# Block transposes of q and k in a fused retention and gated-MLP kernel: TensorE or the DMA queue

## The chip, the cores and the metric

One core of a Trainium2 chip runs the kernel. The metric is device time in microseconds (us) for one execution, the median of the runs; lower is better. The engines are named as in the profile: PE (TensorE), PEld (its weight loads), DVE (VectorE), ACT (ScalarE), POOL (GpSimd) and SP (SyncE, which here only issues DMAs; SPq is its queue).

## The reference

```python
# q, k, v: [8, 8, 576, 64] f32 (batch, heads, positions, head_dim)
scores = q @ k.T / sqrt(64)                       # per batch and head
gamma = 1 - 2 ** (-5 - arange(8))                 # per head
ret = scores * where(i >= j, gamma ** (i - j), 0)
x = (ret @ v) with the heads put side by side     # [8, 576, 512]
h = gelu_tanh(x @ w_in)                           # w_in [512, 1024]
u, v = h[..., :512], h[..., 512:]
v_n = (v - mean) / sqrt(var + 1e-6) * g_ln        # over the 512 columns
v_s = w_sg @ v_n + b_sg                           # over positions, w_sg [576, 576]
out = x + (u * v_s) @ w_out                       # f32
```

## The kernel before, in words

**Blocks.** The sequence work is cut into 18 blocks (`NB`). A block is 256 positions by 8 heads: block 0 of each group of nine takes the first 64 positions of four batches, and the other eight take the two halves of the remaining 512 positions of those four batches. The decay is factored into tables `gq` and `gk`, so that the causal retention becomes a product of scaled q and k, a mask, and a running state.

**Steps of a block j.** `load` brings q, k, v in f32 from HBM, issued on SyncE (L87 and L91; 512 KB each). `cast` scales and converts them to bf16 tiles `qb`, `kb`, `vb`, in the loop on POOL (L245, L263). `T(j, part)` turns a block's q or k: eight TensorE transposes (L272) into one PSUM tile `tp`, and one copy to SBUF, on DVE for `qT` and on ACT for `kT` (both by the helper at L245). `Sc` makes the scores from `kT` and `qT` (L296) and masks them on DVE (L300); it is called in two halves, g = 0 and 1. `Z` updates the state (L321), `inter` applies the earlier state to `qT` (L337), `intra` applies the masked scores to v (L348) and copies the result to `xT` on ACT. `V` and `U` are the two halves of the first MLP matmul with gelu (L365, L414); `V` puts the normalisation off by `later(2, stats)` and `later(4, norm)`. `W` mixes over positions (L434, L436), `O` is the last matmul with the residual (L443, L446), the copy to `ob` on ACT (L449) and the store issued on SyncE (L452, L455).

**Order.** The order is written out by hand, engine queue by engine queue, and nothing reorders it. Blocks 0 to 2 are in a straight prologue, which also transposes blocks 3 and 4. The main loop (L603) runs j from 3 to 17; iteration j works on block j, makes the scores of block j + 1, casts block j + 3, loads block j + 4 and transposes block j + 2: q after the first slot of queued work, k near the end. `W` and `O` steps wait in a list and are put in by `run(slots[i])`, one to two at a time. `tick()` is called at the end of `T`, `V`, `U`, `W` and `O`; every deferred step counts these calls and is put into the queues when its count is out.

**Buffers.** `ld` has three buffers for loads, `w2` two for `qb`, `qT` and `kT`, `w3` three for `kb`, `vb` and `ob`. The PSUM pool `psS` has two tiles of the tag `att`, shared by `tp` and by the scores `sc`.

Of the kernel before, what the change touches and what calls it, by code (L numbers as in the profile page):

```python
# [12 lines left out]
BF = mybir.dt.bfloat16  # L13
# [6 lines left out]
def kernel(  # L20
# [12 lines left out]
    nc = tc.nc  # L33
# [3 lines left out]
    KK = H // 2  # L37
# [4 lines left out]
    NB = B // GB * NPG  # L42
# [7 lines left out]
    w2 = ctx.enter_context(tc.tile_pool(name="w2", bufs=2))  # L50
# [11 lines left out]
    def place(j):  # L62

        gr, w = divmod(j, NPG)
        return (gr, None, 0) if w == 0 else (gr, GB * gr + (w - 1) // 2, (w - 1) % 2)

    def chunk(j, c):

        gr, b, half = place(j)
        if b is None:  # L70
            return 2 * gr + c, MID
        return b // 2, (MID + 1) * (b % 2) + 2 * half + c
# [3 lines left out]
    def load(j, parts=(k, q, v)):  # L76
        if j not in loaded:
            loaded[j] = ld.tile([128, 2, H, 2, D], F32, name="qk"), ld.tile([128, H, 2, D], F32, name="vf")
        qk, vf = loaded[j]
        gr, b, half = place(j)  # L80
        for dst, src in ((qk[:, 1], k), (qk[:, 0], q), (vf, v)):
            if src not in parts:
                continue
            if b is None:
                for x in range(GB):
                    eng = nc.scalar if j == 0 and x >= 2 and src is not v else nc.sync
                    eng.dma_start(dst[32 * x:32 * x + 32], src[GB * gr + x, :, :LEAD, :].rearrange(  # L87
                        "h (p a) d -> p h (a d)", a=2))
            else:
                s0 = LEAD + 256 * half  # L90
                nc.sync.dma_start(dst[:], src[b, :, s0:s0 + 256, :].rearrange("h (p a) d -> p h (a d)", a=2))  # L91
# [143 lines left out]
    def tick():  # L235
        for e in pend:
            e[0] -= 1
        while pend and pend[0][0] <= 0:
            pend.pop(0)[1]()

    blk = {}
    xTs, uTs, gTs, vns, zbs = {}, {}, {}, {}, {}

    def copy(eng, o, i):
        (eng.copy if eng is nc.scalar else eng.tensor_copy)(o, i)  # L245

    def cast(j, part, eng):
        s = blk.setdefault(j, {})
        qk, vf = loaded[j]
        b, half = place(j)[1:]  # L250
        kind = 0 if b is None else 1 + half
        if part == "q":
            dst, src, tab = w2.tile([128, 2, H, D], BF, name="qb"), qk[:, 0], gq
        else:
            pool = consts if b is None else w3
            dst = pool.tile([128, 2, H, D], BF, name=part + ("lead" if b is None else "b"))
            src, tab = (qk[:, 1], gk) if part == "k" else (vf[:], None)
        s[part + "b"] = dst
        o = dst[:].rearrange("p a h d -> p h a d")
        if tab is None:  # L260
            copy(eng, o, src)
        else:
            eng.tensor_tensor(o, src, tab[:, kind].rearrange("p a h -> p h a").unsqueeze(3).to_broadcast(  # L263
                [128, H, 2, D]), op=Alu.mult)

    def T(j, part):
        s = blk[j]
        src = s[part + "b"]
        tp = psS.tile([128, 2, KK, 128], BF, name="tp", tag="att")
        for a in range(2):  # L270
            for kk in range(KK):
                nc.tensor.transpose(tp[:, a, kk, :], src[:, a, 2 * kk:2 * kk + 2, :].rearrange("p h d -> p (h d)"),  # L272
                                    ident[:])
        dst = w2.tile([128, 2, KK, 128], BF, name=part + "T")
        s[part + "T"] = dst
        if j == 0 and part == "q":
            nc.vector.tensor_copy(dst[:, :, :2], tp[:, :, :2])
            nc.scalar.copy(dst[:, :, 2:], tp[:, :, 2:])
        else:
            copy(nc.vector if part == "q" else nc.scalar, dst[:], tp[:])  # L280
        tick()

    def Sc(j, g):
        s = blk[j]
        qT, kT = s["qT"], s["kT"]
        if g == 0:
            s["ret"] = w2.tile([128, 2, KK, 2, 128], BF, name="ret")
        sc = [(psD if (j, g) == (0, 1) else psS).tile([128, 2, 2, 128], F32, name="sc",
                                                      tag="d" if (j, g) == (0, 1) else "att") for _ in range(2)]
        for x in range(2):  # L290
            kk = 2 * g + x
            for a in range(2):
                for r in range(2):
                    for c in range(2):
                        rr, cc = slice(64 * r, 64 * r + 64), slice(64 * c, 64 * c + 64)
                        nc.tensor.matmul(sc[r][cc, x, a, :], kT[rr, a, kk, cc], qT[rr, :, kk, cc],  # L296
                                         start=True, stop=True, skip_group_check=True)
        msk = mask[1 if place(j)[1] is None else 0]
        for r in range(2):
            nc.vector.tensor_tensor(s["ret"][:, r, 2 * g:2 * g + 2], sc[r][:],  # L300
                                    msk[:].unsqueeze(1).to_broadcast([128, 2, 2, 128]), op=Alu.mult)
# [3 lines left out]
    def Z(j, c):  # L305

        gr, b, half = place(j)
        if b is None or (half, c) == (1, 1):
            nb = GB * gr if b is None else b + 1
            if c == 0 or nb == GB * (gr + 1):  # L310
                return
            src, lo, n, first = blk[NPG * gr], 32 * (nb % GB), 32, True
            zcur[0] = psZ.tile([128, KK, D], F32, name="zp")
        else:
            src, lo, n, first = blk[j], 64 * c, 64, False
        z, rows = zcur[0], slice(lo, lo + n)
        for a in range(2):
            for kk in range(KK):
                for r in range(2):
                    h = 2 * kk + r  # L320
                    nc.tensor.matmul(z[64 * r:64 * r + 64, kk, :], src["kb"][rows, a, h, :], src["vb"][rows, a, h, :],  # L321
                                     start=(first and a == 0 and kk == 0), stop=True, skip_group_check=True)
        zb = w3.tile([128, KK, D], BF, name="zb")
        copy(nc.scalar if j < 3 else nc.vector, zb[:], z[:])
        zbs[(j, 1) if c == 0 else (j + 1, 0)] = zb
# [14 lines left out]
    def intra(j):  # L340
        s = blk[j]
        ret, vb, ot = s["ret"], s["vb"], s["ot"]
        ks = [(kk, a) for kk in (2, 3, 0, 1) for a in range(2)]
        for kk, a in ks:
            for c in range(2):
                for r in range(2):
                    cc = slice(64 * c, 64 * c + 64)
                    nc.tensor.matmul(ot[c][64 * r:64 * r + 64, kk], vb[cc, a, 2 * kk + r, :],  # L348
                                     ret[cc, r, kk, a, :],
                                     start=(place(j)[1] is None and (kk, a) == ks[0]),  # L350
                                     stop=True, skip_group_check=True)
        for c in range(2):
            p, m = chunk(j, c)
            if p not in xTs:
                xTs[p] = pairp.tile([128, KK, NT * 128], BF, name="xT")
            x = xTs[p][:, :, 128 * m:128 * m + 128].rearrange("p k (t a) -> p k a t", a=2)
            copy(nc.vector if j < 3 and c == 1 else nc.scalar, x, ot[c][:])
# [102 lines left out]
    def run(n):  # L460
        for _ in range(n):
            if wo:
                wo.pop(0)()
# [139 lines left out]
    for j in range(HEAD, NB):  # L603
        nx = j + 1 < NB
        slots = where[share.get(j, 6)]
        more = (lambda *p: load(j + 4, p)) if j + 4 < NB else (lambda *p: None)
        more(q)
        intra(j)
        if nx:
            Sc(j + 1, 0)  # L610
            Z(j + 1, 0)
        if j + 3 < NB:
            cast(j + 3, "q", nc.gpsimd)
        run(slots[0])
        more(k)
        if j + 2 < NB:
            T(j + 2, "q")
        V(j, 0)
        if not nx:
            V(j, 1)  # L620
        run(slots[1])
        U(j, 0)
        more(v)
        if nx:
            inter(j + 1)
            Sc(j + 1, 1)
            Z(j + 1, 1)
            run(slots[2])
            V(j, 1)
        if j + 3 < NB:  # L630
            cast(j + 3, "k", nc.gpsimd)
            cast(j + 3, "v", nc.gpsimd)
        if j + 2 < NB:
            T(j + 2, "k")
        U(j, 1)
        run(slots[3])
        release(j)
# [36 lines left out]
```

## Time and profile before

| what | value |
|---|---|
| median of 3 runs | 234.67 us (234.17 to 237.1) |
| the profiled execution | 234.34 us, of which 232.6 us span |
| TensorE clock granted | 0.995 of full speed |
| busy share PE, PEld, DVE, ACT, POOL | 92%, 67%, 71%, 58%, 56% |
| PE transposes (L272) | 288, of which 144 of q and 144 of k |
| copies of `kT` (ACT) and `qT` (DVE, L245) | 18 at 1008 ns, 17 at 688 ns |
| DMA | 41.59 MB in 64261 packets, mean 179 GB/s |

The span runs from the first to the last instruction of the profiled execution; a little time lies around it. Busy time of PE overlaps between neighbouring groups, so the place that a group takes in the queue is read from the starts of the groups. A row of the timeline gives start, length, engine, source line, operation, what it writes and reads, and how many instructions were merged. A window row gives the window, its length, and the busy time of PE, PEld, DVE, ACT and POOL with the count of instructions, then the clock, the DMA engines' mean busy share and GB/s. A DMA row gives the size and the median time from issue to landing.

### The profile page before, as it was taken

The page shows a single profiled execution, that of the slowest core. Times are in us where ns is not written, and L with a number is a line of the kernel's source. Part 1 is how long each engine was busy: PE and PEld are TensorE (multiplying, and loading weights), DVE is VectorE, ACT ScalarE, POOL GpSimd, SP SyncE. Part 2 cuts the span into 40 slices and gives each one's busy share as a digit, 9 for nine tenths or more (in the row PEclk, how much of TensorE's full clock was granted, in tenths as well). Part 3 has the DMA queues.
Part 4 walks back from the last instruction along what each step waited for, and adds up shares of the span by engine and source line. Part 5 has one row for each costly group of instructions (what it writes and reads, how often), then busy time and mean ns, then how long its engine had stood idle before and what let it go on. Part 6 is the DMA issues. An engine that isn't in the chain of part 4 may idle for free.

```text
span 232.6 us, 8357 instructions
## 1 busy us (share of the span) xinstructions
PE 215.0 (92%) x3603; PEld 154.8 (67%) x3603; DVE 165.8 (71%) x357; ACT 134.7 (58%) x217; POOL 129.4 (56%) x130
## 2 busy tenths in 40 slices
PE   7796879789997999999999899999999999999991
PEld 3344476577776786777768677777777777667760
DVE  5476788688979896579767886779857985566320
ACT  5353568614669464946575757657394739466332
POOL 5298869799958485538555674939381611113000
PEclk9999999999999999999999999999999999999997
DMA  6999999999396993699249922869522003300344
GB/s 167 286 301 297 302 258 275 238 282 268 94 261 204 201 230 65 207 278 291 79 126 299 276 74 66 251 213 287 146 90 93 4 3 111 118 3 0 136 116 159
DMA packets 64261, 41.59 MB, mean 179 GB/s; under 512 B 2208, under 2 KB 58592, under 8 KB 64224
## 3 DMA queue, kind: packets, MB, share of 16 engines
q1 hardware_dynamic: 61664, 39.33, 62.6%
q0 software_dynamic: 1472, 1.20, 3.1%
q10 hardware_dynamic: 1088, 0.52, 1.0%
q8 instruction: 28, 0.46, 0.9%
q14 instruction: 9, 0.07, 0.1%
HBM read 32.79 MB, written 9.44 MB: 182 GB/s over the span
## 4 chain that ended last, share of the span: by engine, by line
PE 67%; ACT 7%; DVE 6%; DMA 6%; POOL 5%; SPq 5%; issue 1%; ACTq 1%; DVEq 0%; POOLq 0%
PE wp L434 15%; PE op L443 13%; PE hv L365 10%; PE hu L414 10%; PE tp L272 5%; SPq L91 5%; DMA wst<-in_moe_w_in_dram 4%; PE op L446 3%; POOL rs L372 3%; PE zp L321 3%; PE sc L296 3%; PE ot L348 3%; PE ot L337 3%; DMA qk<-in_q_dram 2%; DVE bst L376 2%; ACT vnm L393 2%
## 5 line engine op out<-in xcount | busy, mean ns | idle before, releaser
L372 POOL TENSOR_TENSOR rs<-rs,mhalf 128x1 f32<-128x1 f32 x36 | 33.0, 916 | 73.0 <-DVE rs L380 67.9
L300 DVE TENSOR_TENSOR ret<-sc,mask 128x512 bf16<-128x512 f32 x72 | 46.2, 684 | 12.9 <-PE sc L296 12.8
L434 PE MATMUL wp<-wT,vn 128*128 128x288 bf16 x256 | 41.7, 287 | 2.9 <-ACT vn L397 2.8
L436 DVE TENSOR_TENSOR gT<-wp,uT 128x288 bf16<-128x288 f32 x64 | 28.1, 453 | 16.8 <-PE wp L434 14.0
L365 PE MATMUL hv<-w_in,xT 128*128 128x512 bf16 x144 | 36.5, 379 | 2.4 <-ACT xT L245 2.4
L414 PE MATMUL hu<-xT,w_in 128*128 128x128 bf16 x576 | 37.8, 219 | 0.0
L443 PE MATMUL op<-w_out,gT 128*128 128x512 bf16 x144 | 37.1, 380 | 0.0
L414 PEld LDWEIGHTS <-w_in 128*128 128x128 bf16 x576 | 34.0, 98 | 1.9
L368 ACT ACTIVATE vg<-hv 128x512 f32<-128x512 f32 x36 | 21.4, 596 | 22.5 <-PE hv L365 22.3
L376 DVE BATCH_NORM_STATS2 bst<-vg 128x6 f32<-128x512 f32 x36 | 24.8, 689 | 12.1 <-ACT vg L368 11.9
L449 ACT COPY ob<-op 128x512 f32<-128x512 f32 x36 | 20.9, 586 | 20.5 <-PE op L446 18.0
L263 POOL TENSOR_TENSOR kb<-qk,gk 128x1024 bf16<-128x1024 f32 x16 | 31.1, 1941 | 2.8 <-DMA qk<-in_k_dram 2.8
L397 ACT ACTIVATE vn<-vc,rs 128x512 bf16<-128x512 f32 x32 | 23.1, 722 | 14.4 <-POOL rs L372 12.4
L434 PEld LDWEIGHTS <-vn 128*128 128x128 bf16 x256 | 23.8, 98 | 10.7 <-ACT vn L397 3.7
L385 DVE SCALAR_TENSOR_TENSOR vc<-vg,mv,g_bc 128x512 f32<-128x512 f32 x36 | 29.9, 830 | 0.2 <-issue 0.2
L263 POOL TENSOR_TENSOR qb<-qk,gq 128x1024 bf16<-128x1024 f32 x15 | 28.9, 1929 | 0.0
L417 ACT ACTIVATE uT<-hu 128x512 bf16<-128x512 f32 x36 | 21.7, 602 | 11.5 <-PE hu L414 11.5
L245 ACT CAST xT<-ot 128x512 bf16<-128x512 f32 x33 | 22.0, 733 | 1.8 <-PE ot L348 1.6
L245 ACT COPY kT<-tp 128x1024 bf16<-128x1024 bf16 x18 | 18.1, 1008 | 8.3 <-PE tp L272 8.3
L365 PEld LDWEIGHTS <-xT 128*128 128x128 bf16 x144 | 12.8, 98 | 13.7 <-ACT xT L245 4.0
L443 PEld LDWEIGHTS <-gT 128*128 128x128 bf16 x144 | 12.3, 98 | 9.5
L434 PE MATMUL wp<-wL,vnm 128*128 128x288 bf16 x64 | 18.4, 287 | 0.0
(95 smaller groups left out, 290.0 us busy)
## 6 DMA issues: line engine op xcount, KB each, us to landing
qk<-in_k_dram SPq DMA_DIRECT2D x16, 512.0 KB, 8.2
qk<-in_q_dram SPq DMA_DIRECT2D x16, 512.0 KB, 7.5
vf<-in_v_dram SPq DMA_DIRECT2D x16, 512.0 KB, 7.6
out_dram<-ob SPq DMA_DIRECT2D x32, 256.0 KB, 2.5
wst<-in_moe_w_in_dram SPq DMA_DIRECT2D x2, 1024.0 KB, 7.3
vf<-in_v_dram SPq DMA_DIRECT2D x8, 128.0 KB, 4.3
out_dram<-ob SPq DMA_DIRECT2D x8, 128.0 KB, 2.4
qk<-in_k_dram SPq DMA_DIRECT2D x6, 128.0 KB, 3.4
```

Source lines behind the costliest of these rows:

```text
L245: (eng.copy if eng is nc.scalar else eng.tensor_copy)(o, i)
L263: eng.tensor_tensor(o, src, tab[:, kind].rearrange("p a h -> p h a").unsqueeze(3).to_broadcast([128, H, 2, D]), op=Alu.mult)
L300: nc.vector.tensor_tensor(s["ret"][:, r, 2 * g:2 * g + 2], sc[r][:], msk[:].unsqueeze(1).to_broadcast([128, 2, 2, 128]), op=Alu.mult)
L365: nc.tensor.matmul(hv[:], xTs[p][:, kk, 128 * m:128 * m + 128], w_in[:, kk, F2:], start=(kk == 0), stop=(kk == KK - 1))
L372: nc.gpsimd.tensor_tensor(st["rs"][:], st["rs"][:], mhalf[:], op=Alu.pow)
L376: nc.vector.bn_stats(bst[:], vg[:])
L385: nc.vector.scalar_tensor_tensor(vc[:], vg[:], mv[:, 0:1], g_bc[:], op0=Alu.subtract, op1=Alu.mult)
L397: nc.scalar.mul(vn[:], vc[:], rs[:])
L414: nc.tensor.matmul(hu[:, c, :], w_in[:, kk, 128 * c:128 * c + 128], xTs[p][:, kk, 128 * m:128 * m + 128], start=(kk == 0), stop=(kk == KK ...
L434: nc.tensor.matmul(ps[:], vns[p, m][e][:, 128 * c:128 * c + 128], w, start=(x == 0), stop=(x == SB - 1))
L436: nc.vector.tensor_tensor(gTs[p][:, c, col:col + HS], ps[:], uTs[p][:, c, col:col + HS], op=Alu.mult)
L443: nc.tensor.matmul(op[:], gTs[p][:, c, r], w_out[:, c, :], start=(c == 0), stop=False, skip_group_check=True)
```

## The change

In the main loop both calls of `T` are replaced by a new function `turn`, which issues one DMA on SyncE: a transposing DMA that reads the block's bf16 tile in SBUF and writes `qT` or `kT` in SBUF in the same layout as before. No PSUM tile and no copy is used. For q it stands at the start of iteration j, behind the q load of block j + 4 and ahead of `intra(j)`; for k behind the k load of block j + 4, ahead of `V(j, 0)`. `turn` does not call `tick()`. Iterations 3 to 15 have it, so blocks 5 to 17; the prologue's calls of `T` for blocks 0 to 4 stay.

```diff
+    def turn(j, part):
+
+        s = blk[j]
+        s[part + "T"] = dst = w2.tile([128, 2, KK, 128], BF, name=part + "T")
+        nc.sync.dma_start_transpose(dst[:].rearrange("p a k t -> p (a k) t"),
+                                    s[part + "b"][:].rearrange("p a h d -> p (a h d)"))
...
         more(q)
+        if j + 2 < NB:
+            turn(j + 2, "q")
         intra(j)
...
         run(slots[0])
         more(k)
         if j + 2 < NB:
-            T(j + 2, "q")
+            turn(j + 2, "k")
         V(j, 0)
...
             cast(j + 3, "k", nc.gpsimd)
             cast(j + 3, "v", nc.gpsimd)
-        if j + 2 < NB:
-            T(j + 2, "k")
         U(j, 1)
```

The function T stays as it is for blocks 0 to 4:

```python
    def T(j, part):
        ...
        for a in range(2):
            for kk in range(KK):
                nc.tensor.transpose(tp[:, a, kk, :], src[:, a, 2 * kk:2 * kk + 2, :].rearrange("p h d -> p (h d)"),
                                    ident[:])
        dst = w2.tile([128, 2, KK, 128], BF, name=part + "T")
        ...
            copy(nc.vector if part == "q" else nc.scalar, dst[:], tp[:])
        tick()
```

## The prediction

> **What bounds the kernel now.** I read the busy shares first, then the chain that ended last, then windows of the stage that the edit touches, then the DMA view. The page's busy line, its DMA lines and its chain:
>
> ```profile
> PE 215.0 (92%) x3603; PEld 154.8 (67%) x3603; DVE 165.8 (71%) x357; ACT 134.7 (58%) x217; POOL 129.4 (56%) x130
> ...
> DMA  6999999999396993699249922869522003300344
> GB/s 167 286 301 297 302 258 275 238 282 268 94 261 204 201 230 65 207 278 291 79 126 299 276 74 66 251 213 287 146 90 93 4 3 111 118 3 0 136 116 159
> ...
> PE 67%; ACT 7%; DVE 6%; DMA 6%; POOL 5%; SPq 5%; issue 1%; ACTq 1%; DVEq 0%; POOLq 0%
> ```
>
> TensorE is busy for 92% and carries 67% of the chain; no other engine is near it. The DMA engines are the second full resource: near nine tenths up to about 50 us, then in bursts, at most 302 GB/s, and nearly idle after 170 us. The stage of the edit, in windows (columns: window and length, PE, PEld, DVE, ACT, POOL busy, then clock, DMA share, GB/s):
>
> ```profile
> 62.00:84.00 22.00, 20.75 (x395) 15.61 (x391) 18.81 (x39) 15.30 (x25) 14.95 (x13) 1.00 0.83 205
> 118.30:139.00 20.70, 19.67 (x389) 15.31 (x392) 16.25 (x37) 13.14 (x21) 11.79 (x9) 1.00 0.81 218
> 62.20:172.90 110.70, 108.41 (x1961) 81.20 (x1964) 85.95 (x185) 71.68 (x116) 68.47 (x54) 1.00 0.72 190
> ```
>
> From 62.2 to 172.9 us PE is busy 108.41 of 110.7 us at a clock of 1.00, and what is missing lies in the two shorter windows. So here time is what PE's queue costs, and DMA stands at 0.72. The main loop's length comes from the first and the last of its intra groups in that window:
>
> ```profile
> 62.16 0.64 PE L348 MATMUL ot<-ret,vb 64*64 64x128 bf16 x32
> ...
> 172.80 0.64 PE L348 MATMUL ot<-ret,vb 64*64 64x128 bf16 x32
> ```
>
> Ten iterations lie between these starts: (172.80 - 62.16)/10 = 11.06 us each.
>
> **What is removed.** The loop makes blocks 5 to 17 by `turn`: 13 blocks, q and k, so 26 calls of T go, with 208 PE transposes, 13 DVE copies and 13 ACT copies. What one T holds of PE's queue is the distance from its start to the start of what follows:
>
> ```profile
> 109.04 0.61 PE L272 MATMUL tp<-ident,qb 128*128 128x128 bf16 x8
> 109.49 0.81 PE L365 MATMUL hv<-w_in,xT 128*128 128x512 bf16 x3
> ```
>
> That is 0.45 us for eight transposes (the 0.61 us is busy time that overlaps the next group). 26 x 0.45 = 11.7 us. Not all of it is on the path: in two stretches the chain runs through ACT, DVE and POOL while PE has spare time:
>
> ```profile
> 65.81 0.61 ACT vg L368
> ...
> 75.07 0.91 PE wp L434 x6
> ...
> 123.57 0.61 DVE bst L376
> ...
> 132.39 1.04 PE hv L365 x4
> ```
>
> The windows of the transposes alone (PE, DVE, ACT busy) show how many T lie in these:
>
> ```profile
> 65.80:75.10 9.30, 0.61 (x8) 0.00 (x0) 1.00 (x1) 1.00 0.82 241
> 123.60:132.40 8.80, 1.22 (x16) 0.18 (x1) 1.01 (x1) 1.00 1.12 287
> ```
>
> 8 + 16 transposes, three T, so 3 x 0.45 = 1.35 us gain nothing. The first term is -(11.7 - 1.35) = -10.35 us, bounds -10.35 and -11.7. The 26 copies lie on engines at 71% and 58%; I count no gain for them.
>
> **The lost ticks.** T also called tick(), `turn` does not, so the deferred norm steps come up to two calls later: some `bst` groups stand behind one more `gT` on DVE, and some `vn` behind `xT` or `ob` on ACT. Who waits is the matmul group that reads `vn`:
>
> ```profile
> PE wp L434 <- ACT vn L397: 2.8, 2, 1.5
> ```
>
> These two waits total 2.8 us. I take 0, since DVE and ACT also lose their copies; the bounds are -2.8 (waits gone) and +2.8 (doubled).
>
> **What is added: the transfers.** 26 DMA transposes of 128x1024 bf16, 262,144 bytes each, in SyncE's queue between the loads. The built instruction cuts one into 64 tiles of 16 rows by 128 columns: 1,024 source rows of 256 bytes, and in the destination 8,192 pieces of 32 bytes. No row of this trace is a transpose, so I bound it by other transfers:
>
> ```profile
> q1 hardware_dynamic: 61664, 39.33, 62.6%
> ...
> qk<-in_k_dram SPq DMA_DIRECT2D x16, 512.0 KB, 8.2
> ```
>
> By bytes at the best slice, 262,144 / 302 GB/s = 0.87 us. By pieces: a block's load is 1,024 rows of 512 bytes, 524,288 / 302 GB/s = 1.74 us, or 27 ns a row on each of 16 engines. By the mean packet, 0.626 x 16 x 232.6 us / 61,664 = 37.8 ns, and 64 rows on each engine make 2.42 us. If each 32-byte piece cost 27 ns, 512 per engine make 13.9 us. Ends: 0.87 and 13.9 us. The nearest row is the block's load, with as many pieces and twice the bytes, so I take the middle of 0.87 and 1.74: 1.3 us.
>
> The room: an iteration moves 190 GB/s x 11.06 us = 2.10 MB and uses 0.72 x 11.06 = 7.96 us of the DMA engines by their share, 6.96 us at 302 GB/s. After the edit it would last 11.06 - 0.90 = 10.16 us. That leaves 2.2 to 3.2 us, middle 2.7, for two transposes of 1.3 us, 2.6 us. They just fit, so this term is 0. It eats the whole gain once 11 iterations that still load lose 10.35 us, 0.94 each: at (2.2 + 0.94)/2 = 1.6 to (3.2 + 0.94)/2 = 2.1 us a transpose.
>
> **What is added: a wait.** `turn` stands on SyncE behind the load of the same name and, in some iterations, behind an out store that waits for ACT's `ob`. Queued behind it are the v load, the later stores and the next loads; those have a block and more before POOL wants them. For its own operands it waits on POOL's casts, a block ahead, and on PE's reads of the old buffer. What can be late is kT, which PE wants in `Sc(j+2, 0)` one iteration on. Two iterations in which a store holds the k load back, SyncE's rows, then PE's scores:
>
> ```profile
> 144.41 0.43 SPq L91 DMA_DIRECT2D qk<-in_k_dram  x1
> ...
> 153.57 0.43 SPq L91 DMA_DIRECT2D qk<-in_k_dram  x1
> ```
>
> ```profile
> 150.52 0.39 PE L296 MATMUL sc<-qT,kT 64*64 64x128 bf16 x16
> ...
> 161.48 0.39 PE L296 MATMUL sc<-qT,kT 64*64 64x128 bf16 x16
> ```
>
> Their landing, from the DMA view of each issue:
>
> ```profile
> qk<-in_k_dram SPq DMA_DIRECT2D x1, 512.0 KB, 5.3
> ...
> qk<-in_k_dram SPq DMA_DIRECT2D x1, 512.0 KB, 7.0
> ```
>
> From issue to need there are 6.1 and 7.9 us, less 0.45 us for the T that goes in between: 5.7 and 7.5. If the transpose lands 1.3 us after the load ahead of it, that is 6.6 and 8.3: late by 0.9 and 0.8 us. I take four such iterations at 0.85: +3.4 us; the ends are 0 and 11 x 0.85 = 9.4 us. Elsewhere SyncE runs ahead and the block of lead covers it.
>
> **The sum** is made against the profiled execution: 232.6 us of span, 234.34 us in all, 0.33 below the median of 234.67. 234.34 - 10.35 + 0 + 0 + 3.4 = **227.4 us**. Its own range is 222 to 232.
>
> **The rivals.**
>
> *All is hidden.* kT lands in time everywhere and PE's whole 11.7 us go: 234.34 - 11.7 = 222.6 us. For it speak the median load's 8.2 us, which is queueing with its neighbours rather than work; against it the two rows above.
>
> *The DMA engines become the bound.* At 2.42 us a transpose, two take 4.84 us against 2.2 us of room: 2.6 us over in each of 11 loading iterations, 29 us. 234.34 - 10.35 + 29 = 253 us, slower. It decides from 1.6 to 2.1 us a transpose on; stores and loads then land ever later, and PE waits at the scores and POOL at its casts. For it: the share of 1.12 at 287 GB/s in one window, and the first 50 us. Against it: half the bytes per row, and idle engines after 170 us.
>
> *Transposes cost by small pieces.* At 13.9 us each, two take 27.8 us against 2.7: 25.1 x 11 = 276 us, about 500 us in all. Every smaller per-piece cost above the 2.42 us lies between this and 253. Nothing in the trace excludes it, since no transfer here writes 32-byte runs. A rule of the Trainium skill points this way: VectorE: DVE Perf Modes, section "The three transpose paths", has 1309 ns for a 128x128 DMA transpose against 390 ns on TensorE. Eight of them one after another would be an estimated 10.5 us and the kernel about 425 us; no run here shows whether a part of that is a fixed cost paid once.
>
> *The change doesn't do what it says:* the built program has the 26 transposes on SyncE and 208 fewer on PE, so I give this no chance.
>
> **How the numbers follow.** The forecast has 0.45, all hidden 0.13, the DMA bound 0.28, small pieces 0.14. A kernel change here can be told from none at about 2%, 4.7 us. Faster by that is below 230.0: 0.33 of the forecast's 0.45 and all of the first rival, 0.46. Within 2%: the forecast's slow end, 0.12, and the DMA bound's fast end, 0.05, together 0.17. Slower: 0.23 and 0.14, 0.37. Both signs hold much, so the range is wide: 220 us, a little under all hidden, to 275 us, which leaves out the small pieces and little else. The likeliest case's own is 222 to 232.
>
> **What would show it.** Right: the transposes of `tp` end at block 4 (80 PE transposes left), PE's iteration near 10.2 us, landings of `qT` and `kT` of 2 to 8 us, PE waits on `kT` of 0.5 to 1.5 us in about four iterations, a DMA share near 0.9 from 62 to 160 us. Wrong: landings of 10 us and more, long issues on SyncE, PE waiting at L303 in every iteration, or POOL waiting on loads; then the term at fault is the 1.3 us. If PE's iteration stays near 11 us with no such waits, the 0.45 us was not on the path.

## The result, and the profile after

| kernel | median | ratio to before, 95% interval |
|---|---|---|
| before | 234.9 us (20 runs) | |
| the change | 234.41 us (20 runs) | 0.9945 [0.9918, 0.9971] |

The change gains 0.55%, 1.3 us: by the 2% of this measurement, no difference. The ratio, here and below, leaves out the runs that are over 1.5% above the fastest of the same kernel, so it is not the quotient of the medians, here 0.998; gains in us are the ratio's distance from 1 times 234.9. The forecast was 227.4 us. The profile shows that the work did leave PE and that the time came back as waits. The profiled execution of the change took 239.14 us, the longest of its 20, so its waits are at the upper end; the run with a fourth `ob` buffer below has 9.4 us of the same waits in an execution of 233.0 us of span.

The page's busy line, clock line and chain of the change:

```profile
PE 211.0 (89%) x3395; PEld 146.1 (62%) x3395; DVE 159.3 (67%) x344; ACT 123.4 (52%) x204; POOL 129.4 (55%) x130
...
PEclk9999799999999999998899989997999999999999
...
PE 53%; DMA 21%; DVE 8%; POOL 6%; ACT 3%; issue 3%; SPq 3%; ACTq 1%; POOLq 0%; DVEq 0%
```

PE has 208 matmuls fewer (3395 for 3603) but a larger share of idle time, the DMA share of the chain went from 6% to 21%, and the clock, flat before, has dips. Where PE waits now, from the view of waits (engine and line, what ended the wait, us in total, times, longest):

```profile
PE sc L303 <- DMA kT<-kb: 8.7, 5, 2.4
PE sc L303 <- DMA kT<-klead: 2.6, 1, 2.6
PE wp L441 <- ACT vn L404: 2.0, 2, 1.4
```

Six times the scores wait for kT, 11.3 us in all. The kernel before has no such row. What the transfers cost, from the DMA view of the change:

```profile
q1 hardware_dynamic: 89120, 46.15, 87.5%
...
qT<-qb SPq DMA_TRANSPOSE x13, 6.7
kT<-kb SPq DMA_TRANSPOSE x12, 6.1
```

27,456 packets more than before, 1,056 a transpose, and (0.875 x 237.4 - 0.626 x 232.6)/26 = 2.39 us of all 16 engines for one, against 1.3 us in the forecast. This is the sum of the packets' times, and packets overlap: the same share is above 1 in the windows below. So 2.39 us is not the time by which a transpose makes the queue longer. A transpose lands 6.1 to 6.7 us after its issue in the median. One of the waits in order of time, SyncE first and then PE:

```profile
124.34 3.32 SPq L287 DMA_TRANSPOSE qT<-qb  x1
127.75 0.53 SPq L462 DMA_DIRECT2D out_dram<-ob  x1
128.33 0.43 SPq L91 DMA_DIRECT2D qk<-in_k_dram  x1
128.85 3.41 SPq L287 DMA_TRANSPOSE kT<-kb  x1
```

```profile
131.42 0.65 PE L441 MATMUL wp<-wT,vn 128*128 128x288 bf16 x4
132.00 0.64 PE L355 MATMUL ot<-ret,vb 64*64 64x128 bf16 x32
135.00 0.42 PE L303 MATMUL sc<-qT,kT 64*64 64x128 bf16 x16 [2.35 <-DMA kT<-kb]
135.24 0.54 PE L328 MATMUL zp<-vb,kb 64*64 64x64 bf16 x16
135.71 0.42 PE L441 MATMUL wp<-wL,vnm 128*128 128x288 bf16 x1
135.93 1.17 PE L441 MATMUL wp<-wT,vn 128*128 128x288 bf16 x4
```

The issue of the q transpose holds SyncE for 3.32 us, then come a store and the k load, and the k transpose is issued only 3.8 us before PE has nothing left to do (132.64). It lands 6.1 us after its issue, 2.35 us late. After the wait four `wp` matmuls take 1.17 us, where as many took 0.65 us ahead of it: the clock is down for some microseconds. Windows of the change (columns as before; the last three are clock, DMA share and GB/s):

```profile
62.00:84.00 22.00, 18.48 (x351) 13.16 (x350) 16.89 (x36) 12.42 (x21) 13.88 (x12) 1.00 1.20 250
107.00:118.00 11.00, 8.42 (x126) 5.49 (x125) 6.27 (x15) 3.50 (x6) 4.24 (x5) 0.84 1.37 209
...
135.40:140.00 4.60, 4.60 (x47) 2.94 (x38) 2.54 (x5) 0.66 (x2) 0.57 (x1) 0.63 1.17 284
140.00:145.00 5.00, 5.00 (x113) 3.81 (x114) 4.59 (x12) 2.48 (x5) 3.56 (x3) 1.00 1.28 197
```

The three longest waits, 2.58, 2.35 and 2.28 us, are each followed by such a stretch; those of 1.55 and 1.62 us, both in the first row, are not. Between 107 and 173 us four windows have a lower clock: 0.84 in 11 us, 0.92 in 21, 0.92 in 11 and 0.93 in 12. Each length times what its clock lacks to 1 gives 5.2 us in all, an estimate of what the clock cost in this execution if PE was the limit in all of them.

### The profile page after: what moved, and what is told of

Read it like the earlier page. It is cut to its first block, busy times and chain, and to the rows that moved or that the text cites. A ratio compares the mean times of both kernels' runs of the same rounds, so it can differ in the third digit from the quotient of the medians.

```text
span 237.4 us, 7964 instructions
## 1 busy us (share of the span) xinstructions
PE 211.0 (89%) x3395; PEld 146.1 (62%) x3395; DVE 159.3 (67%) x344; ACT 123.4 (52%) x204; POOL 129.4 (55%) x130
## 4 chain that ended last, share of the span: by engine, by line
PE 53%; DMA 21%; DVE 8%; POOL 6%; ACT 3%; issue 3%; SPq 3%; ACTq 1%; POOLq 0%; DVEq 0%
PE wp L441 13%; PE op L450 12%; DMA kT<-kb 10%; PE hv L372 9%; PE hu L421 7%; DMA qk<-in_q_dram 4%; DMA qk<-in_k_dram 4%; DMA kT<-klead 3%; PE op L453 3%; DVE bst L383 3%; PE sc L303 3%; PE zp L328 2%; PE ot L355 2%; DVE vc L392 2%; SPq L91 2%
## 5 line engine op out<-in xcount | busy, mean ns | idle before, releaser
L441 PE MATMUL wp<-wT,vn 128*128 128x288 bf16 x256 | 44.3, 299 | 2.3 <-ACT vn L404 2.0
L372 PE MATMUL hv<-w_in,xT 128*128 128x512 bf16 x144 | 38.0, 391 | 1.4 <-ACT xT L245 1.4
L421 PEld LDWEIGHTS <-w_in 128*128 128x128 bf16 x576 | 34.6, 98 | 5.0
L441 PEld LDWEIGHTS <-vn 128*128 128x128 bf16 x256 | 24.7, 101 | 12.2 <-ACT vn L404 3.2
L392 DVE SCALAR_TENSOR_TENSOR vc<-vg,mv,g_bc 128x512 f32<-128x512 f32 x36 | 31.7, 880 | 0.2 <-issue 0.2
L303 PE MATMUL sc<-qT,kT 64*64 64x128 bf16 x576 | 17.0, 219 | 12.1 <-DMA kT<-kb 8.7
L424 ACT ACTIVATE uT<-hu 128x512 bf16<-128x512 f32 x36 | 21.4, 596 | 11.6 <-PE hu L421 11.3
L372 PEld LDWEIGHTS <-xT 128*128 128x128 bf16 x144 | 13.8, 102 | 14.4 <-ACT xT L245 2.9
L303 PEld LDWEIGHTS <-kT 64*64 64x64 bf16 x576 | 11.8, 106 | 14.9 <-DMA kT<-kb 9.5
L441 PE MATMUL wp<-wL,vnm 128*128 128x288 bf16 x64 | 19.1, 299 | 0.4 <-DVE gT L443 0.4
```

The costliest lines, as they stand in the source:

```text
L372: nc.tensor.matmul(hv[:], xTs[p][:, kk, 128 * m:128 * m + 128], w_in[:, kk, F2:], start=(kk == 0), stop=(kk == KK - 1))
L392: nc.vector.scalar_tensor_tensor(vc[:], vg[:], mv[:, 0:1], g_bc[:], op0=Alu.subtract, op1=Alu.mult)
L421: nc.tensor.matmul(hu[:, c, :], w_in[:, kk, 128 * c:128 * c + 128], xTs[p][:, kk, 128 * m:128 * m + 128], start=(kk == 0), stop=(kk == KK ...
L441: nc.tensor.matmul(ps[:], vns[p, m][e][:, 128 * c:128 * c + 128], w, start=(x == 0), stop=(x == SB - 1))
```

## The experiments

Three theories went in. A: the gain on PE is real and is given back by a late kT. B: the DMA engines are full, so the transfers slow everything, wherever they are issued. C: the transposes were not on the path.

**No transfer.** What the PE work alone is worth.

```diff
...
-        s[part + "T"] = dst = w2.tile([128, 2, KK, 128], BF, name=part + "T")
-        nc.sync.dma_start_transpose(dst[:]..., s[part + "b"][:]...)
+        blk[j][part + "T"] = blk[j - 2][part + "T"]
```

> The changed kernel without its 26 DMA transposes: from block 5 on the scores read the qT and kT tiles of blocks 3 and 4 again, so the output leaves the blocks' own transposed q and k out. It shows what the removed TensorE work is worth when nothing is late. Theory A (the gain is real and is given back in PE's waits for kT and in the lower clock after them): 222.6 to 225 us, 10 to 12 below before, clock 0.99, no wait of PE at the scores. Theory B (the extra transfers fill the DMA engines): the same 222.6 to 225. Theory C (the PE transposes were not on the path, DVE and POOL set the pace): 231 to 235 us.

Measured: 224.94 us, 0.9576 [0.952, 0.9632], clock 1.00, no wait of PE for kT. That is 4.2%, 10.0 us of 234.9, with the 26 copies and the ticks gone as well; theory C falls.

**Transfers that nobody waits for.** T stays everywhere; the transposes run beside it into dead halves of the load buffers.

```diff
+        old = loaded[j][0][:, 0 if part == "q" else 1].rearrange("p h a d -> p (h a d)").bitcast(BF)
+        nc.sync.dma_start_transpose(old[:, :1024]..., blk[j][part + "b"][:]...)
```

> All PE transposes and copies of the kernel before, and beside them the 26 DMA transposes at the places of the change, written into load buffers that are already used up, so that nobody computes with them. (The load that fills that buffer next waits for them.) Theory A: the transfers alone cost little, 234 to 237 us. Theory B: loads and stores are pushed back and the kernel slows by 5 to 12 us, 240 to 247 us, with POOL waiting for loads or ACT for stores. Theory C says nothing of it: 234 to 236 us.

Measured: 238.18 us, 1.010 [1.0024, 1.0176]: 1.0%, some 2.4 us, between A and B and far from B's 5 to 12. The DMA queue is as full as with the change, and the loss shows at the stores (lines of the DMA view and of the waits of this run):

```profile
q1 hardware_dynamic: 89120, 46.15, 90.1%
```

```profile
ACT ob L455 <- DMA out_dram<-ob: 5.0, 4, 1.8
```

ACT waited 0.9 us for stores in the kernel before and 5.0 us here. There are three `ob` buffers, and a store that lands later holds ACT.

**q alone, k alone.** Half of the change each; the other half stays on PE.

```diff
 # q alone
-            turn(j + 2, "k")
...
+            T(j + 2, "k")
 # k alone
-            turn(j + 2, "q")
...
             turn(j + 2, "k")
+            T(j + 2, "q")
```

> Only q goes by DMA, at the place of the change; k stays on PE and ACT as before. 13 transposes of 0.45 us leave PE. Theory A: q stands early in its iteration and lands in time, so half of the gain stays, 5 us: 228 to 231 us, clock 0.99, PE's waits for qT under 2 us in all. Theory B: half of the transfers, half of the loss: 232 to 234 us. Theory C: 232 to 235 us.

> The mirror of q alone: only k goes by DMA, at the place of the change; q stays on PE and DVE. The same 13 transfers and the same 13 x 0.45 us of PE work less as in the run with q alone, which gained 2.5 per cent. Theory A (k's place makes it late): PE waits for kT again, 4 to 11 us, and the kernel takes 231 to 235 us. Theory B (only the count of transfers matters): the same as with q alone, 228 to 230.5 us.

Measured: q alone 229.19 us, 0.9747 [0.9698, 0.9796], with no wait of PE for qT. k alone 231.47 us, 0.9839 [0.98, 0.9877]; the waits for kT in this run:

```profile
PE sc L303 <- DMA kT<-kb: 2.6, 3, 0.9
```

The same 13 transfers and the same PE work gain 2.5% at q's place and 1.6% at k's, and only k's has a wait, so place counts, as A says. (The halves also take their copies off different engines, 13 off DVE for q and 13 off ACT for k; that was not separated.) But the halves together would give 4.1%, and both at once give 0.55%. Without the q transpose ahead of it kT is late by 2.6 us in all, with it by 11.3: what each transpose gains is paid back by what the two together make late.

**Both early.** Same transfers, both ahead of the loads and of the stores of the iteration's slots.

```diff
-        more(q)
         if j + 2 < NB:
             turn(j + 2, "q")
+            turn(j + 2, "k")
+        more(q)
         intra(j)
...
-            turn(j + 2, "k")
```

> Both DMA transposes stand at the start of the iteration, q first, ahead of all three loads of block j + 4 and of the out stores of its slots. The transfers are the same. Theory A: kT is issued some 3 to 6 us earlier and lands before the scores; PE's waits for it go from 11.3 us to under 3, clock 0.99, and the kernel takes 224 to 228 us. Theory B: the DMA engines are as full as before, 232 to 235 us, with the wait moved to the loads. Theory C: 232 to 235 us with no waits at the scores.

Measured: 233.53 us, 0.9824 [0.9754, 0.9893]. The wait for kT is nearly gone, as A had it. The time is unclear: the four runs reach from 230.3 to 236.35 us, between A's band and B's. The waits of the profiled one, 235.45 us, and then ACT and PE about the longest of them:

```profile
PE wp L441 <- ACT vn L404: 6.1, 3, 4.2
...
ACT ob L456 <- DMA out_dram<-ob: 6.0, 3, 4.0
...
PE sc L303 <- DMA kT<-kb: 0.5, 1, 0.5
```

```profile
152.39 0.59 ACT L456 COPY ob<-op 128x512 f32<-128x512 f32 x1 [4.04 <-DMA out_dram<-ob]
152.87 1.32 ACT L245 CAST xT<-ot 128x512 bf16<-128x512 f32 x2
154.03 0.62 ACT L456 COPY ob<-op 128x512 f32<-128x512 f32 x1
154.50 0.76 ACT L404 ACTIVATE vn<-vc,rs 128x512 bf16<-128x512 f32 x1
```

```profile
155.31 0.42 PE L441 MATMUL wp<-wT,vn 128*128 128x288 bf16 x1 [4.17 <-ACT vn L404]
155.52 0.45 PE L441 MATMUL wp<-wL,vnm 128*128 128x288 bf16 x1
155.76 1.91 PE L372 MATMUL hv<-w_in,xT 128*128 128x512 bf16 x4
```

A store lands late, ACT cannot write `ob`, `vn` stands behind it on ACT, and PE waits 4.17 us for `vn`. So in this run the wait moved. Whether the two runs near 231 us have it too is not shown.

**Both early and a fourth `ob` buffer,** with its two controls.

```diff
+    obp = ctx.enter_context(tc.tile_pool(name="obp", bufs=4))
...
-        ob = w3.tile([128, DM], F32, name="ob")
+        ob = obp.tile([128, DM], F32, name="ob")
```

> Both transposes early as in the run before, and four buffers for ob in place of three. With both early PE's wait for kT was gone, and in its place ACT waited 4.0 us once for a store to land before it could write ob, with vn and PE's matmuls behind it. Theory A: this wait was the last large one; it goes, clock 0.99, 226 to 229 us. Theory B (the DMA engines are simply full): the wait shows again elsewhere, at POOL's casts or PE's scores, 231 to 235 us.

> The kernel before with four buffers for ob in place of three, nothing else: the control for the run with both transposes early and four buffers. ACT waited 0.9 us in all for stores in the kernel before, so all theories expect 233 to 236 us, a ratio of 0.995 to 1.002.

> The change in its own places, with four buffers for ob. If the place of kT is the cause and the fourth buffer only removes the wait that follows when kT is early: PE's waits for kT stay near 11 us and the time is that of the change, 233 to 236 us. If the fourth buffer alone brought the gain of the run with both: 228 to 231 us.

| kernel | three `ob` | four `ob` |
|---|---|---|
| before | 1 | 0.9982 [0.994, 1.0023] |
| the change | 0.9945 [0.9918, 0.9971] | 0.9981 [0.9935, 1.0027] |
| both early | 0.9824 [0.9754, 0.9893] | 0.9724 [0.9668, 0.9779] |

The buffer alone does nothing that can be told from noise, before or with the change; the place alone brings 1.8%, unclear against the 2%; both bring 2.8%, 229.02 us. The intervals of the last two overlap, so that both together are faster is shown, and how much of it is the buffer's is not. The waits of both early with four buffers, and of the change with four:

```profile
ACT ob L457 <- DMA out_dram<-ob: 1.4, 1, 1.4
...
PE sc L304 <- DMA kT<-kb: 0.3, 1, 0.3
```

```profile
PE sc L304 <- DMA kT<-kb: 7.7, 4, 2.5
...
PE sc L304 <- DMA kT<-klead: 1.7, 1, 1.7
```

In the first, kT's and the store's waits are both nearly gone, and PE's waits for `vn` still total 4.4 us; in the second, 9.4 us of waits for kT remain. With q alone (229.19 us) it is the best that was run with the whole output; the two are not told apart.

**Stores issued by ACT.** SyncE no longer waits for `ob`.

```diff
...
-            nc.sync.dma_start(out[2 * p + (m > MID), s0:s0 + 128, :], ob[:])
+            nc.scalar.dma_start(out[2 * p + (m > MID), s0:s0 + 128, :], ob[:])
```

> The changed kernel with its out stores issued by ACT, right behind the copy that fills ob, in place of SyncE. The transposes keep their places between the loads, but nothing on SyncE waits for ob any more, and the stores no longer share its queue. Theory A1 (kT is late because its transpose stands behind out stores that wait for ob): SyncE runs ahead, PE's waits for kT fall from 11.3 us to under 3, and the kernel takes 226 to 230 us; ACT pays about 40 issues of 0.4 us, 16 us more busy time at a share of 52 per cent. Theory A2 (kT is late because its data move behind the k load's and v load's in full DMA engines, whoever issues): the waits stay near 11 us and the time within 233 to 237.

Measured: 236.14 us, 1.0038 [1.0, 1.0076]. PE's wait for kT is gone altogether, and SyncE now runs so far ahead that it waits 36.5 us at the transposes for PE to read the old buffer (1.7 us in the change). So the place behind the stores made kT late, as A1 says. But the time is A2's, since ACT now waits at its own issues:

```profile
PE wp L441 <- ACT vn L404: 6.4, 3, 3.2
...
ACT vn L404 <- DMA qT<-qb: 4.4, 1, 4.4
```

In the second row ACT has ended the copy to `ob` at 65.4 us and issues its store only at 69.3 us, with `vn` behind it. The view puts the wait down to a transpose in flight; why the store's issue should wait for one is not shown.

**Filling the wait.** Is the lower clock after each wait a loss of its own?

```diff
+        if g == 0 and j in (5, 7, 9, 11, 13):
+            for _ in range(9):
+                nc.tensor.matmul(sc[0][:]..., w_in[:, 0, :128], w_in[:, 0, :512], start=True, stop=True, ...)
```

> The changed kernel with nine extra matmuls of w_in, 128x512, ahead of the scores of blocks 5, 7, 9, 11 and 13, the ones that waited 1.5 to 2.6 us for kT; the scores overwrite what they write. They fill the wait with about 1.9 us of work each. If the lower clock after these waits is part of the loss (theory A with the clock): clock 0.99 in place of 0.97, and 1 to 4 us less than the change, 230 to 233 us. If the clock costs nothing: 234 to 237 us, equal to the change or a little above, since the filling is not free where kT was less late.

Measured: 235.12 us, 0.9993 [0.9965, 1.0021], clock 1.00 in the profiled execution. The clock came back and the time did not: the kernel is half a per cent above the change. But the filling was far from exact. In the change block 6 waited too and was not filled, and block 7 waited only 0.88 us. In this run's trace kT lands 0.1 to 1.8 us after a filling begins, so of the 10.0 us of the five fillings some 5 us ran when kT was already there, and came on top of PE's queue. The run takes away the lower clock and adds about as much work, so it does not tell what the clock costs. It shows only that fillings of a fixed length do not pay here.

**Fewer bytes.** The change without the v loads from block 7 on.

```diff
...
-            if src not in parts:
+            if src not in parts or (src is v and j >= 7):
                 continue
```

> The change without the v loads from block 7 on: POOL casts an older block's v again, so the output leaves those blocks' own v out. 512 KB less per block for the DMA engines; the queue ahead of each kT transpose (out stores, k load, qT transpose) stays as it is. If kT is late by its place in SyncE's queue: its landing stays near 6 us, PE's waits for it stay at 7 to 11 us, and the time is 231 to 235 us. If full DMA engines make it late: landing 4 to 5 us, waits under 4 us, 227 to 230 us.

Measured: 231.99 us, 0.9885 [0.9818, 0.9951]. The waits and the landing of kT (min, median, max):

```profile
PE sc L304 <- DMA kT<-kb: 5.2, 3, 1.9
...
PE sc L304 <- DMA kT<-klead: 1.5, 1, 1.5
```

```profile
DMA to landing us min/median/max: 3.1/6.2/7.6
```

The landing did not change (6.1 us in the change), as the place theory has it; the waits fell to 6.7 us, just below its band, and the time lies in it. Taking away a third of the block loads from block 7 on helps (1.15%), but less than moving both transposes with a fourth `ob` does (231.99 against 229.02 us). Whether the fewer bytes help or the fewer issues on SyncE, which go with them, was not separated.

**The ticks given back.** Both early, four `ob`, and `turn` calls `tick()`.

> Both transposes early, four buffers for ob, and turn calls tick() as T did, so the deferred norm steps stand where they stood before. If the lost ticks cost nothing, as the prediction had it: 227.5 to 230.5 us, as without. If they make vn late (PE waited 4.4 us for vn in that run, 2.8 us in the kernel before): those waits fall below 3 us and the time to 226 to 228 us.

Measured: 231.33 us, 0.987 [0.9811, 0.9929], a miss for both: the ticks make it slower by 1.5%. The wait for `vn` fell to 2.6 us, but kT is late again by 3.9 us and POOL waits for q loads, 13.1 us against 3.2 without ticks:

```profile
POOL qb L264 <- DMA qk<-in_q_dram: 13.1, 9, 2.6
```

Why the loads are later with the ticks stays open. In this version, then, the lost ticks are no loss; on the change in its own places it was not tried.

## Why the prediction was wrong, step by step

- **What bounds the kernel** was right: PE's queue. 80 transposes of `tp` are left, as said.
- **The first term,** -10.35 us, was right: 10.0 us measured without transfers.
- **The lost ticks,** 0, stand as far as was tried: giving them back did not help.
- **The transfers,** 0, were a little too low: transfers that nobody waits for cost 2.4 us. The 1.3 us for one, "so I take the middle of 0.87 and 1.74: 1.3 us", has two answers. By packet times one takes 2.39 us, next to the 2.42 us by the mean packet that the prediction had put into a rival. But both are sums of overlapping packets, and the rival's 29 us did not come: at a share of 90% in this queue PE still ran almost undisturbed. By landing it was near: at the six waits kT lands 0.8 to 2.4 us after the k load ahead of it, 1.3 us in the mean. That the mean meets the forecast is partly luck, since 1.3 was the middle between two prices of other transfers. What fails is the step from the share to room in the queue and to lost time.
- **The wait,** +3.4 us, is the term that decided, and it was too small. The prediction's first place, the k load at 144.41 us, in the change, SyncE's rows and PE's:

```profile
149.87 0.45 SPq L91 DMA_DIRECT2D qk<-in_k_dram  x1
150.41 3.10 SPq L287 DMA_TRANSPOSE kT<-kb  x1
```

```profile
157.68 0.42 PE L303 MATMUL sc<-qT,kT 64*64 64x128 bf16 x16 [2.28 <-DMA kT<-kb]
```

PE is ready at 155.40, 5.5 us after the k load (5.7 forecast), and starts 7.8 us after it (6.6 forecast): 2.3 us late for 0.9. The second place, at 153.57 us before, has no wait. The landings at the first place, from the DMA view of each issue:

```profile
qk<-in_k_dram SPq DMA_DIRECT2D x1, 512.0 KB, 5.4
...
kT<-kb SPq DMA_TRANSPOSE x1, 7.2
```

The load lands at 155.3 us and the transpose 2.3 us later, where the forecast had 1.3; at four of the other waits it is about 1 us. So "if the transpose lands 1.3 us after the load ahead of it" is not the step that decided. The steps that failed are "I take four such iterations at 0.85" and "Elsewhere SyncE runs ahead and the block of lead covers it". There were six waits of 1.9 us in the mean, 11.3 us, above even the 9.4 us of the term's upper end, and five of them lie elsewhere, at blocks 5, 6, 7, 9 and 11. What the prediction put at nothing, without a row for it, is that the issue of a transpose holds SyncE: 72 us for the 26 issues in this trace, 41 of them for q. It had named long issues only as a sign of being wrong. SyncE no longer runs far ahead: it waits for `ob` at the stores for 55 us in all, where it waited for 115 us before, and the k loads go out later. From k load to need the six blocks had 6.1 to 13.1 us in the kernel before, 8.2 in the mean; in the change they have 4.3 to 7.2 us, 5.3 in the mean, and the k load alone takes 5.0 to 7.1 us to land. In time: -10.0 + 2.4 would be -7.6 us, measured were -1.3, so a late kT, with the lower clock behind the longer waits, costs some 6.3 us. That is a difference of runs, not a measurement by itself, and how it divides between wait and clock is open. Moving both transposes ahead, with a fourth `ob`, brings -6.5 us and so recovers most of it.
- **The rivals.** None of them came as described. The DMA-bound one met the packet time of a transpose and was wrong in its consequence; small pieces at 13.9 us are excluded by landings of 3.1 us. There the Trainium skill's rule, VectorE: DVE Perf Modes, section "The three transpose paths", has 1309 ns for one 128x128 transpose; eight in sequence would be 10.5 us, and here a transpose of eight such blocks lands in 3.1 us when the queue is quiet (the minimum of the landing row of the run without v loads), so the eight are not paid one after another. Whether most of that figure is a cost paid once, or the blocks run side by side, no run here separates.

## What to carry to other kernels

Work moved from a full engine to the DMA queue is worth its PE time only where the result has slack, and slack must be counted in the queue as it will be: every issue ahead of it holds the issuing engine, here for 1.2 to 6.9 us a transpose, and two new transfers in a row delay each other. Put such transfers ahead of bulk loads and of stores that wait, or move only the half that has the longer lead: q alone gained 2.5% where both gained 0.55%. When a wait goes and the time stays, look for the next buffer that is written late; in the profiled run here it was the output's. When you fill a wait to keep the clock up, look in the trace when the awaited tile lands: half of the filling here came after it.

## What was not expected of the hardware

- A DMA transpose of 128x1024 bf16 from SBUF to SBUF holds SyncE between 1.23 and 6.87 us. Issue times in the change, ns min/median/max:

```profile
L287 SPq DMA_TRANSPOSE kT<-kb x12: 1233/2152/3413, 59.9 to 189.1; - x12
```

```profile
L287 SPq DMA_TRANSPOSE qT<-qb x13: 1287/3203/6874, 52.3 to 186.5; - x13
```

The four after 181 us, where no loads are left, take 1.23 to 1.53 us and land 3.1 to 3.4 us after their issue. Between loads all but two take 1.9 us and more, and the medians of landing are 6.1 and 6.7 us. That a full queue is what lengthens the issue fits this and is not shown.
- A wait of 2.35 us is enough to lower PE's clock: four `wp` matmuls took 1.17 us after it and 0.65 us before, and the granted clock is 0.63 from 135.4 to 140 us. Waits of 2.28 and 2.58 us did the same, one of 1.62 us did not. The Trainium skill, TensorE: Matmul & The Clock Gate, section "Why this matters for your kernels", warns of PE-idle gaps over some 3 us; here a shorter one did it.
